# Attention into a channel-mixing block: unread products, one early load, and a third issuer of DMAs at the start

## The chip, the cores and the metric

The kernel runs on one core of a Trainium2 chip. The metric is the device time of one execution in microseconds (us). Before the change three runs gave a median of 1044.69 us (1044.38 to 1045.98). All times of rows below come from one profiled execution of the same program.

## The reference, cut to what matters

Four batches, 12 heads, 448 tokens, 64 channels a head. Scores are mixed over the heads by a 12x12 matrix ahead of the softmax, and the probabilities by another one behind it. What comes out goes through a low-rank token mixing and a two-layer channel mixing of width 3072.

```
scores = einsum('bhij,hg->bgij', q @ k.T / 8, w_pre)      # B=4, H=12, S=448, D=64
attn   = softmax(scores, axis=-1)
attn   = einsum('bhij,hg->bgij', attn, w_post)
x      = (attn @ v) as (B, S, 768)
u      = x + (x.T @ U @ V).T                              # rank 32
out    = u + relu(u @ w_ch1) @ w_ch2                      # 768 -> 3072 -> 768
```

## The kernel before, in words

The attention is cut into 17 units (`UNITS`): a unit holds some tokens of one batch, ten tokens to a chunk. The units of batch 0 have 6, 6, 12, 12 and 9 chunks; they are numbered from 0, so the "third unit" is unit 2. The work of one unit goes through these steps, and each name is that of the step in the code:

- `q` and `k` are loads. Units 0 and 1 have small q tiles (unit 0 in two loads, unit 1 in one); from unit 2 on there are two loads of three head pairs each. The k of batch 0 comes in three loads, `("k", 0, 0)`, `("k", 0, 2)` and `("k", 0, 4)`.
- `qk` multiplies q and k (line 435). For units 0 and 1 one step does four heads, so a unit has three steps; from unit 2 on a step does two heads and a unit has six.
- `qk_out` copies the scores from the PSUM bank to SBUF (lines 340 or 342, on ScalarE or VectorE).
- `relay` is a DMA, one for each head of a unit (line 456). It takes the rows of one head and spreads them over every twelfth partition of the tile `t`, so that the heads of one token lie in neighbouring partitions. There are two tiles `t`; units 0 and 2 share one, unit 1 has the other. GpSimd clears the first partitions of both at the start (line 396).
- `premix` multiplies `t` by the head matrix (line 495), two chunks to a step, so units 0 and 1 have three steps each (0 to 2 and 3 to 5), and unit 2 begins with step 6. A premix needs all twelve relays of its unit.
- `max` (VectorE), `exp` (ScalarE), `eps` (GpSimd), `recip` (VectorE) and `scale` (GpSimd) make the softmax and the scaled second head matrix; `postmix` (line 531) applies it, `post_out` copies, and `av` (lines 572 and 580) multiplies by v.

Behind the attention come the low-rank step, then the channel mixing in seven products for each 2x2 block (line 1026) and the last matmuls (line 1134).

A planner (`Plan.order`) writes down the order of every engine's instructions when the program is built. Each step has a rank, the steps that it needs, the slots that it holds, and the engines that may run it with a cost for each. The planner steps through its own time; a free engine takes the ready step of lowest rank, and where several engines may run a step, it goes to the one that would end it first. The program then has, on every engine, the order that came out. The constants of `RANK` are in units of chunks: premix step k has rank 2k. `k0` and `kstep` set the ranks of `qk` of units 0 and 1, and through these the ranks of their loads, copies and relays.

Before the change the relays of unit 0 may be issued by SP or by ScalarE (`SHARED = 1`), those of all other units by SP alone. The two q loads of unit 2 have ranks of -8.3 and -3.3 and need premix step 0.

`warm` are products of a zeroed tile with itself that nobody reads (line 484): a first block of three (`WARM[0]`), ahead of the first `qk`, and a second of five behind the last `qk` of unit 1, ahead of premix step 0. The tile `blank` is zeroed by VectorE (line 486). A float32 product of 448 columns is two matmul instructions in the trace, so the blocks have 6 and 10.

Of the kernel before, what the change touches and what calls it, by code (L numbers as in the profile page):

```python
# [18 lines left out]
B, H, S, D = 4, 12, 448, 64  # L19
# [13 lines left out]
QA, QW = 4, 124  # L33
# [11 lines left out]
class Unit:  # L45
# [10 lines left out]


RANK = dict(
    e0=-97.289, estep=7.59, er=4.323, qk_lead=4.915, qk_step=0.84, av_off=3.794, av_step=0.935, post=4.408,
    kr=0.705, vr=1.125, qr=6.14, mx=0.587, ex=0.852, ep=1.625, po=3.145, qo=1.135, uv0=6, uvs=-0.052, uv1=2.315,  # L60
    raw=5.564, k0=-12.826, kstep=0.571, m0=12.258, pu=1.842, ev=29.543, lead=14.607, t0=-4.815, ts=0.56,
    t1=2.158, ta=31.914, tb=3.344, dl=32.545, hl=13.674, out=3,
)

# [3 lines left out]


SHARED = 1  # L70
WARM = 3, 5
WEIGHT = {("POOL", "ACT"): 1.0, ("POOL", "DVE"): 3.221, ("DVE", "POOL"): 0.8, ("ACT", "DVE"): 1.3}


# [16 lines left out]
def words(ap):  # L91
    return ap.bitcast(I32).rearrange("p (n t) -> p n t", t=2)
# [165 lines left out]
def build(tc, q2, kt, vj, wpre_in, wpost_in, u_in, v_in, ident, w1j, w2, out, show=None):  # L258
# [5 lines left out]
    def pool(ctx, name, bufs, side="left", **kw):  # L264
        sb[name] = Pool(ctx.enter_context(tc.tile_pool(name=name, bufs=1, side=side, **kw)), plan.where)
        return sb[name]
# [5 lines left out]
    plan = Plan({**BUFS, **CAPS, "t": 2}, CAPS, 4, WEIGHT)  # L272
# [12 lines left out]
    p = pool(uv_ctx, "c", 1)  # L285
# [86 lines left out]
    def OUT(n):  # L372
        return [("ACT", 55 + 0.833 * n), ("DVE", 75 + 1.042 * n)]
# [7 lines left out]
    chunks, first = [], {}  # L381
# [17 lines left out]
    def rank_qk(u, h):  # L399
        if u == 0:  # L400
            return RANK["k0"] + h * RANK["kstep"]
        if u == 1:
            return RANK["k0"] + (h + 12) * RANK["kstep"]
        return first[u] - RANK["qk_lead"] - (11 - h) * RANK["qk_step"]

    def rank_av(u, p):
        return first[u + 1] + RANK["av_off"] + p * RANK["av_step"]
# [29 lines left out]
    def lent(u, p):  # L437

        n = sum(H // 2 // units[v].pairs for v in range(u)) + p // units[u].pairs
        return n if n < 9 else None  # L440
# [18 lines left out]
    for u, un in enumerate(units):  # L459
        b, size = un.b, 128 * (H // 2) * un.cols  # L460
        src = q2[at:at + size].rearrange("(p h i) -> p h i", p=128, h=H // 2)
        at += size
        at_q, hold = [], [("qk", 0, 4)] if u == 1 else []
        for p, n in Q_LOADS[min(u, 2)]:
            at_q += [p] * n
            plan.add(("q", u, p), [("SP", (430, 200 * n * un.cols // QW))], partial(load_q, u=u, p=p, n=n, src=src), rank_qk(u, 2 * p) - RANK["qr"], [("premix", first[u - 2] // 2)] if u > 1 else (), [("q", u)])
        for p in range(0, H // 2, un.pairs):
            r = rank_qk(u, 2 * p)
            o, s = ("qk", (u, p)), [("s", (u, p))] if lent(u, p) is None else []
            plan.add(("qk", u, p), [("PE", 760)], partial(qk, u=u, p=p), r, [("q", u, at_q[p]), *hold, *{("k", b, x) for x in (([p // 2 * 2]) if b == 0 else range(p, p + 1))}],  # L470
                     [o, ("q", u), ("k", b)])
            plan.add(("qk_out", u, p), OUT(2 * S), partial(qk_out, u=u, p=p), r + RANK["qo"], [("qk", u, p)], [o] + s, port=())
            for h in range(2 * p, 2 * (p + un.pairs)):
                cost = (800, 1000 * un.n // H)
                plan.add(("relay", u, h), [("SP", cost)] + [("ACT", cost)] * (u < SHARED), partial(relay, u=u, h=h), r + RANK["qo"], [("qk_out", u, p)], s + [("t", u)])


    def blank():
        return sb["xn"].tile([JP, NJ, LW], F32R, "xh", ("xn", "blank")).bitcast(F32).rearrange("p j n -> p (j n)")
# [3 lines left out]
        for _ in range(n):  # L483
            eng.matmul(o[:64, 0, :S], lhsT=z[:, S:S + 64], rhs=z[:, :S], start=True, stop=True)

    plan.add("blank", [("DVE", 700)], lambda eng: eng.memset(blank(), 0.0), -30, (), [("xn", "blank")])
    for i, n in enumerate(WARM):
        plan.add(("warm", i), [("PE", 760 * n)], partial(warm, i=i, n=n), (-30, -1)[i], ["blank"] + [[], [("qk", 1, 4), ("qk", 0, 4)]][i], [("pre", ("warm", i)), ("xn", "blank")])

# [51 lines left out]
    for k in range(NC // 2):  # L541
        r = 2 * k
        us = sorted({chunks[2 * k][0], chunks[2 * k + 1][0]})
        pre, post, st, e, wr = ("pre", k), ("post", k), ("st", k), ("e", k), ("wr", k)
        ts = [("t", u) for u in us]
# [8 lines left out]
        for js in ([(0, 1)] if len(us) == 1 else [(0,), (1,)]):  # L554
            u = chunks[2 * k + js[0]][0]
# [40 lines left out]
    for u, un in enumerate(units):  # L596
# [3 lines left out]
        for p in range(0, H // 2, AV):  # L600
            r = rank_av(u, p)
# [226 lines left out]
    for b in range(B):  # L828
        us = of_batch[b]
        RB = first[us[-1] + 1] + RANK["uv0"]  # L830
        for k in range(KC // 2):
            r = RB + 2 * RANK["uvs"] * k
            tp, tr, hp, xn, t3 = ("lr", ("tp", b, k)), ("lr", ("tr", b, k)), ("lr", ("hp", b, k)), ("xn", (b, k)), ("t3", (b, k))
# [20 lines left out]
    def when(F, p, j):  # L854
        return U0 + PU * (7 * nth[F, p] + POS[j])
# [32 lines left out]
    for p in range(2):  # L888
        b0, b1 = 2 * p, 2 * p + 1
        gates = [[None] + ["open_qk"] * 3 + ["open_t1"] * 2 + ["open_mix"], ["open_tail", "open_x1", "open_x0", "open_uv", "open_uv", "open_x2", "open_x3"]][p]  # L890
        for i in range(3):
            lo, hi = i, i + 3
            u = {(x, y): [("keep", (b0, b1)[y], (lo, hi)[x] // 2)] for x in range(2) for y in range(2)}
# [57 lines left out]
    for F in range(NF):  # L951
        r = [when(F, 0, j) - RANK["lead"] for j in range(7)]
# [3 lines left out]
        for i, f, h, j in pieces:  # L956
            key = ("w", F, i)
            src = words(w1j[2 * F + f][:, h * HW:(h + 1) * HW])
# [86 lines left out]
    for n, (F, p) in enumerate(chains):  # L1045
# [8 lines left out]
        ev = [when(F, p, j) - RANK["ev"] for j in range(7)]  # L1054
        q, s, c11, = ("hs", (n, "q")), ("hs", (n, "b")), ("hs", (n, "a"))
# [19 lines left out]
    def due(f, b, c=0):  # L1075
        return D0 + GS * group[f] + 2 * PU * (3 * b + c / 2)
# [19 lines left out]
    for f in range(KF):  # L1096
        for b in range(B):
            r = due(f, b) - RANK["hl"]
# [10 lines left out]
        for i in range(2):  # L1109
            key = ("v", f, i)  # L1110
            r = due(f, 0, 4 * i) - RANK["dl"]
            k, ka = 7 * NF + 2 * f + i, 5 * NF + 2 * f + i
            src = words(w2[f * 128:(f + 1) * 128, :][:, i * HW:(i + 1) * HW])
# [29 lines left out]
    for g, fs in enumerate(GROUPS):  # L1143
        for b in range(B):
            n = 1 if (g, b) == (NGR - 1, B - 1) else 2
            for c in range(0, KC, n):
                r = due(fs[0], b, c)
# [83 lines left out]
```

## Time and profile before

| | |
|---|---|
| median of three runs | 1044.69 us |
| profiled execution | 1043.51 us |
| its span, first to last instruction | 1041.7 us |
| TensorE busy | 1002.3 us, 96% |
| VectorE, ScalarE, GpSimd busy | 790.3, 467.5, 356.4 us |
| mean granted TensorE clock | 0.995 |

The profiled execution took 1.8 us beside its span. The busy share of TensorE is a mean: it is 74% to 88% in the six stretches of ten us from the start, and 99% from 500 us on. The table is read with that in mind: what a change at the start is worth is seen in the first 60 us.

### The profile page before, as it was taken

How to read it: one execution, taken by the hardware profiler on the slowest of the kernel's cores; microseconds unless marked ns; L12 is line 12 of the kernel's file. 1: busy time of each engine (PE TensorE's matmuls, PEld its weight loads, DVE VectorE, ACT ScalarE, POOL GpSimd, SP SyncE). 2: the span in 40 equal slices, each digit the busy share in tenths (PEclk: the TensorE clock that was granted, in tenths of full speed). 3: DMA queues.
4: the chain of work that ended last, by engine and by line, in shares of the span. 5: the costliest groups of instructions: out<-in, count | busy, mean ns of one | idle time of the engine just before them, and what ended most of it. 6: DMA issues, size and time to landing. Idle time of an engine off the chain costs nothing.

```text
span 1041.7 us, 28885 instructions
## 1 busy us (share of the span) xinstructions
PE 1002.3 (96%) x12044; PEld 840.2 (81%) x12044; DVE 790.3 (76%) x1194; ACT 467.5 (45%) x970; POOL 356.4 (34%) x461
## 2 busy tenths in 40 slices
PE   7889999999899897999999999999999999999998
PEld 2566666666566686989999999999999999999997
DVE  3375685687676779799999987894999999996223
ACT  2667767777777763444433333431333333420000
POOL 4121121223211675655565543450432413422000
PEclk9899999999999999999999999999999999999999
DMA  5755657677574233344544544686353454440023
GB/s 177 235 160 183 192 187 203 199 240 215 170 244 153 62 107 120 109 143 151 151 152 148 160 136 136 202 277 241 101 171 117 131 181 139 151 140 1 1 83 130
DMA packets 89499, 161.34 MB, mean 155 GB/s; under 512 B 10696, under 2 KB 72088, under 8 KB 89368
## 3 DMA queue, kind: packets, MB, share of 16 engines
q1 hardware_dynamic: 88948, 158.84, 47.9%
q8 instruction: 95, 1.56, 0.6%
q10 hardware_dynamic: 420, 0.65, 0.2%
q14 instruction: 36, 0.29, 0.1%
HBM read 86.14 MB, written 34.60 MB: 116 GB/s over the span
## 4 chain that ended last, share of the span: by engine, by line
PE 58%; DVE 4%; ACT 0%; issue 0%; ACTq 0%; DVEq 0%
PE bank L1134 33%; PE bank L1026 25%; DVE aw L720 1%; DVE aw L721 0%; DVE acc L875 0%; DVE x L726 0%; DVE u L347 0%; DVE aw L875 0%; DVE aw L716 0%; DVE x L725 0%; DVE hs L1039 0%; DVE acc L822 0%; DVE w L347 0%; DVE hs L342 0%; DVE xl L347 0%
## 5 line engine op out<-in xcount | busy, mean ns | idle before, releaser
L1134 PE MATMUL bank<-u,w 128*128 128x448 f32 x1728 | 345.9, 362 | 0.0
L1134 PEld LDWEIGHTS bank<-u,w 128*128 128x128 f32 x1728 | 324.0, 187 | 21.6
L1026 PE MATMUL bank<-u,w 128*128 128x448 f32 x1512 | 307.0, 364 | 7.6 <-DVE hs L1039 2.9
L1026 PEld LDWEIGHTS bank<-u,w 128*128 128x128 f32 x1512 | 284.0, 188 | 28.6 <-POOL w L347 3.3
L1137 DVE TENSOR_TENSOR acc<-acc,bank 128x896 f32<-128x896 f32 (+1 forms) x99 | 104.3, 1054 | 78.5 <-PE bank L1134 78.4
L730 POOL TENSOR_TENSOR aw<-aw,x 128x384 f32<-128x384 f32 x74 | 83.4, 1126 | 205.9 <-DVE x L726 202.2
L347 POOL TENSOR_TENSOR w<-aw,w 128x384 fp32r<-128x384 f32 x84 | 99.0, 1185 | 90.7 <-ACT w L340 88.6
L531 PEld LDWEIGHTS bank<-wr,e 60*64 60x64 f32 x5040 | 91.1, 136 | 44.3 <-issue 30.6
L507 ACT ACTIVATE e<-bank,st 128x448 f32<-128x448 f32 x180 | 113.1, 638 | 26.6 <-DVE st L513 13.0
L502 DVE TENSOR_REDUCE st<-bank 128x2 f32<-128x896 f32 x90 | 97.4, 1085 | 33.7 <-PE bank L495 32.5
L340 ACT CAST w<-aw 128x384 fp32r<-128x384 f32 x102 | 52.1, 515 | 140.9 <-PE bank L1134 68.3
L709 ACT ACTIVATE x<-kr 128x384 f32<-128x384 f32 x82 | 45.6, 556 | 127.2 <-DMA kr<-in_w 99.1
L531 PE MATMUL bank<-wr,e 60*64 60x60 f32 x5040 | 94.1, 220 | 8.2 <-issue 5.9
L435 PE MATMUL bank<-k,q 64*64 64x448 f32 (+1 forms) x768 | 92.9, 549 | 5.8 <-DMA q<-in_q 2.5
L495 PE MATMUL bank<-t,wpre 64*64 64x448 f32 x720 | 86.8, 546 | 8.6 <-DMA v<-in_vj 2.6
L510 POOL TENSOR_SCALAR st<-st 128x2 f32<-128x2 f32 x90 | 17.9, 199 | 189.4 <-ACT e L507 188.4
L340 ACT COPY hs<-bank 128x448 f32<-128x448 f32 x87 | 46.3, 534 | 74.5 <-PE bank L1026 70.0
L1094 DVE SCALAR_TENSOR_TENSOR u<-hs,u 128x448 fp32r<-128x448 f32 x96 | 78.9, 852 | 0.0
L340 ACT COPY a<-bank 128x840 f32<-128x840 f32 (+1 forms) x72 | 60.5, 845 | 35.2 <-PE bank L531 35.2
L721 DVE SCALAR_TENSOR_TENSOR aw<-x,aw 128x384 f32<-128x384 f32 x88 | 67.5, 767 | 6.6
L572 PEld LDWEIGHTS bank<-a,v 128*64 128x64 f32 x1224 | 57.4, 139 | 13.5 <-ACT a L340 4.2
L726 DVE SCALAR_TENSOR_TENSOR x<-kr,x 128x384 f32<-128x384 uint32 (+2 forms) x99 | 64.1, 647 | 3.4
(72 smaller groups left out, 1019.2 us busy)
## 6 DMA issues: line engine op xcount, KB each, us to landing
hd<-hs SPq DMA_DIRECT2D x96, 224.0 KB
hs<-hd SPq DMA_DIRECT2D x96, 224.0 KB
t<-s SPq DMA_DIRECT2D x102, 210.0 KB
kr<-in_w1j SPq DMA_DIRECT2D x48, 384.0 KB
kr<-in_w SPq DMA_DIRECT2D x48, 384.0 KB
v<-in_vj SPq DMA_DIRECT2D x24, 256.0 KB
q<-in_q SPq DMA_DIRECT2D x30, 186.0 KB
ud<-acc SPq DMA_DIRECT2D x12, 448.0 KB
```

Source lines behind the costliest of these rows:

```text
L340: eng.copy(out=o, in_=i)
L347: eng.tensor_tensor(out=o, in0=a, in1=b, op=ALU.subtract)
L435: eng.matmul(o[at, i, :S], lhsT=q[d, pj, of], rhs=k[d, pj, :], start=True, stop=True)
L495: eng.matmul(o[64 * j:64 * j + 64, i, :S], lhsT=wpre[64 * i:min(64 * i + 64, QW)], rhs=tt[side(u)][64 * i:min(64 * i + 64, QW), n, :], sta ...
L502: eng.tensor_reduce(out=mx, in_=T["pre", k][:, :, :S], axis=AX.X, op=ALU.max, negate=True)
L507: eng.activation(out=e[:, i], in_=T["pre", k][:, i, :S], func=ACTF.Exp, bias=T["mx", k][:, i:i + 1], accum_out=sm[:, i:i + 1])
L531: eng.matmul(d, lhsT=e[64 * j:64 * j + HALF, i, x * KB:x * KB + KB], rhs=wr[64 * j:64 * j + HALF, i].rearrange("p (g m) -> p g m", m=MH), ...
L730: eng.tensor_tensor(out=f32(a), in0=f32(a), in1=f32(x), op=ALU.add)
L1026: eng.matmul(o, lhsT=w[:, x, i * 128:(i + 1) * 128], rhs=u[:, i, y, :], start=j < 2 and i + t == 0, stop=i + t == 4, skip_group_check=True)
L1094: eng.scalar_tensor_tensor(out=h[:, 1, :], in0=T["hr", f, b], scalar=0.0, in1=f32(h[:, 0, :]), op0=ALU.max, op1=ALU.subtract)
L1134: eng.matmul(ps[:, j, :S], lhsT=w[:, x, cc * 128:(cc + 1) * 128], rhs=h, start=(i == 0), stop=(i == len(todo) - 1))
L1137: eng.tensor_tensor(out=two(b, c, n), in0=two(b, c, n), in1=T.pop(("dn", g, b, c))[:, :n, :S], op=ADD)
```

## The change

Three things at the start of the program, and a few constants of the planner:

- The blocks of unread products have two and three products in place of three and five, and only the 512 columns of `blank` that they read are zeroed, in place of 1024.
- The q loads of unit 2 get the rank just behind the relays of unit 0's last four heads, and need `qk_out` of these heads in place of premix step 0.
- The relays of units 1 and 2 may be issued by GpSimd too, at a cost of 1050 ns to the planner (SP's is 800).
- `k0` and `kstep` move the ranks of `qk` of units 0 and 1 from -12.8 ... -1.4 to -8.5 ... 0.2. The ranks of the first loads follow, and with these the order in which SP asks for them: q of unit 1 and the head matrix now stand ahead of the first and the second k load.
- `av_step`, `ex` and `po` shift the ranks of `av`, `exp` and `post_out` by 0.011 a pair, 0.006 and 0.039.

```diff
-    ... av_off=3.794, av_step=0.935, post=4.408,
-    kr=0.705, vr=1.125, qr=6.14, mx=0.587, ex=0.852, ep=1.625, po=3.145, qo=1.135, ...
-    raw=5.564, k0=-12.826, kstep=0.571, ...
+    ... av_off=3.794, av_step=0.924, post=4.408,
+    kr=0.705, vr=1.125, qr=6.14, mx=0.587, ex=0.858, ep=1.625, po=3.106, qo=1.135, ...
+    raw=5.564, k0=-8.529, kstep=0.437, ...
...
-WARM = 3, 5
+BY_POOL = 1, 2
+WARM = 2, 3
...
-            plan.add(("q", u, p), ..., rank_qk(u, 2 * p) - RANK["qr"], [("premix", first[u - 2] // 2)] if u > 1 else (), [("q", u)])
+            plan.add(("q", u, p), ..., rank_qk(0, 11) + RANK["qo"] + 0.01 if u == 2 else rank_qk(u, 2 * p) - RANK["qr"],
+                     [("premix", first[u - 2] // 2)] if u > 2 else [("qk_out", 0, 4)] if u == 2 else (), [("q", u)])
...
-                plan.add(("relay", u, h), [("SP", cost)] + [("ACT", cost)] * (u < SHARED), ...
+                plan.add(("relay", u, h), [("SP", cost)] + [("ACT", cost)] * (u < SHARED) + [("POOL", (1050, cost[1]))] * (u in BY_POOL), ...
...
-    plan.add("blank", [("DVE", 700)], lambda eng: eng.memset(blank(), 0.0), ...
+    plan.add("blank", [("DVE", 400)], lambda eng: eng.memset(blank()[:, :S + 64], 0.0), ...
```

## Rows read from the trace of the kernel before

**Rows 1.** The page: TensorE's busy time, and the last chain's shares by engine.
```profile
PE 1002.3 (96%) x12044; PEld 840.2 (81%) x12044; DVE 790.3 (76%) x1194; ACT 467.5 (45%) x970; POOL 356.4 (34%) x461
...
PE 58%; DVE 4%; ACT 0%; issue 0%; ACTq 0%; DVEq 0%
```

**Rows 2.** Waits of TensorE, 0 to 60 us: us in total, times, longest.
```profile
PE bank L495 <- DMA v<-in_vj: 2.6, 1, 2.6
PE bank L435 <- DMA q<-in_q: 2.5, 1, 2.5
PE bank L495 <- DMA t<-acc: 2.1, 1, 2.1
```

**Rows 3.** The same view, 60 to 420 us, its largest entry.
```profile
PE bank L531 <- issue: 4.4, 7, 1.6
```

**Rows 4.** Timeline to 20 us: start, duration (us), instructions, idle time before and releaser.
```profile
0.72 9.08 POOL L396 MEMSET t<- 4x5376 f32 x2 [0.29 <-POOLq L1219]
...
1.01 0.91 DVE L486 MEMSET xh<- 112x1024 f32 x1 [1.01 <-PEq L1219]
...
1.98 4.74 PE L484 MATMUL bank<-xh 112*64 112x448 f32 x6 [1.98 <-DVE xh L486]
...
2.28 0.70 SPq L418 DMA_DIRECT2D q<-in_q  x1
...
6.65 1.34 PE L435 MATMUL bank<-k,q 64*64 64x448 f32 x8
...
8.51 4.26 PE L435 MATMUL bank<-k,q 64*64 64x448 f32 x40 [0.53 <-DMA k<-in_kt]
...
8.99 12.09 SPq L456 DMA_DIRECT2D t<-acc  x13
9.00 6.04 ACTq L456 DMA_DIRECT2D t<-acc  x6
...
12.71 3.97 PE L484 MATMUL bank<-xh 112*64 112x448 f32 x10
...
18.78 2.49 PE L495 MATMUL bank<-t,wpre 64*64 64x448 f32 x24 [2.10 <-DMA t<-acc]
```

**Rows 5.** Timeline from 20 to 46 us.
```profile
21.12 0.95 SPq L418 DMA_DIRECT2D q<-in_q  x2
...
23.75 2.59 PE L435 MATMUL bank<-k,q 64*64 64x448 f32 x16 [2.48 <-DMA q<-in_q]
...
24.89 0.91 ACT L340 COPY acc<-bank 124x896 f32<-124x896 f32 x1 [0.76 <-PE bank L435]
...
26.10 1.72 PE L531 MATMUL bank<-wr,e 60*64 60x60 f32 x56
...
26.77 5.29 SPq L456 DMA_DIRECT2D t<-acc  x6
...
27.58 1.84 PE L435 MATMUL bank<-k,q 64*64 64x448 f32 x16
...
29.25 0.99 PE L531 MATMUL bank<-wr,e 60*64 60x60 f32 x56
...
32.81 5.29 SPq L456 DMA_DIRECT2D t<-s  x6
...
43.80 2.17 PE L495 MATMUL bank<-t,wpre 64*64 64x448 f32 x16 [2.59 <-DMA v<-in_vj]
```

**Rows 6.** Busy time by stretches of 1 us; last: granted clock, DMA share, GB/s.
```profile
4.00:5.00 1.00, 1.00 (x2) 0.23 (x1) 0.00 (x0) 0.00 (x0) 1.00 (x1) 1.00 1.01 355
...
17.00:18.00 1.00, 0.00 (x0) 0.00 (x0) 0.00 (x0) 0.00 (x0) 0.00 (x0) 1.00 0.61 212
...
26.00:27.00 1.00, 1.00 (x40) 0.90 (x36) 0.00 (x0) 0.61 (x1) 0.00 (x0) 0.50 0.49 142
```

**Rows 7.** The same view, stretches of 10 us.
```profile
20.00:30.00 10.00, 7.52 (x156) 4.08 (x152) 4.25 (x7) 6.88 (x16) 1.74 (x6) 0.83 0.60 180
...
40.00:50.00 10.00, 7.41 (x143) 4.31 (x135) 2.85 (x5) 6.05 (x13) 0.48 (x2) 0.83 0.91 272
```

More of the change, by code (lines that the diff above doesn't have):

```diff
@@ L58 @@
 RANK = dict(
-    e0=-97.289, estep=7.59, er=4.323, qk_lead=4.915, qk_step=0.84, av_off=3.794, av_step=0.935, post=4.408,
-    kr=0.705, vr=1.125, qr=6.14, mx=0.587, ex=0.852, ep=1.625, po=3.145, qo=1.135, uv0=6, uvs=-0.052, uv1=2.315,
-    raw=5.564, k0=-12.826, kstep=0.571, m0=12.258, pu=1.842, ev=29.543, lead=14.607, t0=-4.815, ts=0.56,
+    e0=-97.289, estep=7.59, er=4.323, qk_lead=4.915, qk_step=0.84, av_off=3.794, av_step=0.924, post=4.408,
+    kr=0.705, vr=1.125, qr=6.14, mx=0.587, ex=0.858, ep=1.625, po=3.106, qo=1.135, uv0=6, uvs=-0.052, uv1=2.315,
+    raw=5.564, k0=-8.529, kstep=0.437, m0=12.258, pu=1.842, ev=29.543, lead=14.607, t0=-4.815, ts=0.56,
     t1=2.158, ta=31.914, tb=3.344, dl=32.545, hl=13.674, out=3,
@@ L465, in build @@
             at_q += [p] * n
-            plan.add(("q", u, p), [("SP", (430, 200 * n * un.cols // QW))], partial(load_q, u=u, p=p, n=n, src=src), rank_qk(u, 2 * p) - RANK["qr"], [("premix", first[u - 2] // 2)] if u > 1 else (), [("q", u)])
+            plan.add(("q", u, p), [("SP", (430, 200 * n * un.cols // QW))], partial(load_q, u=u, p=p, n=n, src=src), rank_qk(0, 11) + RANK["qo"] + 0.01 if u == 2 else rank_qk(u, 2 * p) - RANK["qr"],
+                     [("premix", first[u - 2] // 2)] if u > 2 else [("qk_out", 0, 4)] if u == 2 else (), [("q", u)])
         for p in range(0, H // 2, un.pairs):
@@ L474, in build @@
                 cost = (800, 1000 * un.n // H)
-                plan.add(("relay", u, h), [("SP", cost)] + [("ACT", cost)] * (u < SHARED), partial(relay, u=u, h=h), r + RANK["qo"], [("qk_out", u, p)], s + [("t", u)])
+                plan.add(("relay", u, h), [("SP", cost)] + [("ACT", cost)] * (u < SHARED) + [("POOL", (1050, cost[1]))] * (u in BY_POOL), partial(relay, u=u, h=h), r + RANK["qo"], [("qk_out", u, p)], s + [("t", u)])
     def blank():
@@ L484, in warm @@
             eng.matmul(o[:64, 0, :S], lhsT=z[:, S:S + 64], rhs=z[:, :S], start=True, stop=True)
-    plan.add("blank", [("DVE", 700)], lambda eng: eng.memset(blank(), 0.0), -30, (), [("xn", "blank")])
+    plan.add("blank", [("DVE", 400)], lambda eng: eng.memset(blank()[:, :S + 64], 0.0), -30, (), [("xn", "blank")])
     for i, n in enumerate(WARM):
```

## The prediction

> **What bounds the kernel now.** I read the page first, for the engine that is the limit and for where the last chain goes, then the waits of TensorE, then the timeline around the largest of them, then stretches for the clock and the transfers. TensorE is busy 96% of the span and carries 58% of the last chain, VectorE 4% [rows 1]: whatever lets TensorE do the same work earlier shows in the end time. In the first 60 us three waits for transfers stand out, 2.1, 2.5 and 2.6 us [rows 2]; from there to 420 us no entry is over 4.4 us, and that one is seven pieces of at most 1.6 [rows 3]. The edits lie at those three waits.
>
> The timeline tells what they are. TensorE ends the unread products and waits 2.10 us for the relays of unit 0 (premix 0 at 18.78). It ends the three premixes at 21.27 and waits 2.48 us for q of unit 2, which SP asked for only at 21.12, behind thirteen relays from 8.99 on [rows 4, 5]. And it waits 2.59 us ahead of the first premix of unit 2 at 43.80 [rows 5]. The releaser named there is a v load, but a premix reads no v; it reads `t`, so what is late is unit 2's relays, issued by SP from 26.77 to 38.10.
>
> Two more things have a price. In the two stretches of ten us that hold the waits of 2.48 and 2.59 us, the granted clock is 0.83 [rows 7]: 1.7 us each at the level of 1.2 GHz. The first is seen in the work: sixteen qk matmuls take 2.59 us where the next sixteen take 1.84, and a postmix 1.72 us where the next takes 0.99 [rows 5], 1.48 us together. And while relays run alone the DMA engines are busy 0.61 of 16, at 212 GB/s; loads reach 1.01 and 355 GB/s [rows 6]. A relay writes ten partitions, and 0.61 of 16 engines is ten: these ten are near full.
>
> **The change part by part.** All times are against the profiled run, 1043.51 us (span 1041.7 and 1.8 beside it), which is 1.2 us under the median of 1044.69.
>
> *The q loads of unit 2.* Behind six relays of unit 0 at 12.09/13 = 0.93 us each, SP comes to them at 8.99 + 5.6 = 14.6 in place of 21.12. They landed 2.6 us behind the issue before (23.75 - 21.12); even if their packets queue behind unit 0's last relay, to 18.78, they are there 2.6 - 0.95 later, at 20.5, ahead of the end of the premixes. So the 2.48 us go, hidden behind the premixes. What is late next is the chain max, exp, scale: with qk of unit 2 earlier, TensorE comes to postmix 0 earlier and may wait there.
>
> *Relays of unit 1 by GpSimd.* GpSimd is free when its two memsets end at 9.80 [rows 4]. No row shows a DMA issued by GpSimd. From below I bound an issue by SP's 5.29/6 = 0.88 us [rows 5], from above by twice ScalarE's 6.04/6 = 1.01 [rows 4], and take 1.01, the nearest issue by an engine that also computes. SP then has about six relays of unit 1 in place of twelve, 5 us less, and is no longer late for unit 2: the copy for its first relay ended at 24.89 + 0.91 = 25.80 and SP issued it at 26.77 [rows 5]. That is 0.97 us, and it goes.
>
> The other side: relays of unit 1 begin while unit 0's are in flight, now out of a third queue. From the first copies of unit 1, about 13, to the landing of unit 0's last relay ahead of 18.78, ScalarE's six had half of ten engines nearly full. With a third sharer, what is left of them, some 4 us, may take half as long again at worst: 0 to 2 us on premix 0. I take 0.7.
>
> The Trainium skill speaks against the change here (DMA: Bandwidth & Descriptors, Issuing engines are not separate DMA queues): DMAs of SP, ScalarE and GpSimd run on the same 16 engines and interleave, so several issuers save issue time only. The 0.61 that holds while two queues issue agrees. By the rule alone, the gain is that of the transfer-bound rival below; by the row on SP's late issue, it is mine.
>
> *Relays of unit 2 by GpSimd.* SP needed 11.3 us for twelve; two issuers need half, so issue is no longer the limit, and the transfers are. Of the 2.59 us ahead of premix 6, between 0 (transfers bound) and all may go. I take 1.0, since the stretch at 26 us has the engines at 0.49 [rows 6]: a fifth of their time was free for want of issues.
>
> On GpSimd, `eps` and `scale` now queue behind relays that wait for a `qk_out`. Each relay in front of them delays a postmix by an issue (1.01) or more. I cost it at nothing: until 43.80 TensorE has the wait for unit 2's relays as cover. If that goes, one or two such delays come to 1 to 2 us.
>
> *Order of the first loads.* q of unit 1, 192 KB, goes ahead of the first k load, at the 355 GB/s of this time [rows 6] 0.55 us. The second and third k have the same bytes ahead of them as before. So qk starts later, but the next qk, waiting for k at 8.51 [rows 4], does not. Bounds 0 and 0.55; I take 0.3, for the first relays leave later.
>
> *Unread products and memset.* One product less ahead of qk and a memset half as long free TensorE from its first block at about 4.7 in place of 6.7 (4.74 us for six matmuls, 0.79 each, two fewer, and 0.45 us sooner [rows 4]), but k lands no sooner: no gain. The pace of 0.79 against 3.97/10 = 0.40 in the second block is that of the lower clock. With less work ahead, qk may run at it for longer: 1.34 us for eight matmuls against 0.85 (4.26/5 [rows 4]), 0.5 us each for two or three steps. It hides behind the issue of unit 0's relays, which have 5.6 us of issue from the first on; without that cover it is 1 to 1.5 us. The second block is 1.6 us shorter (two products of 0.79), so the wait ahead of premix 0 grows from 2.10 to 3.7 us. Behind 2.10 us idle the premixes ran at full pace, 24 in 2.49 us; behind 2.48 us the clock fell. So I let the first 1.48 us of slow work move from qk to the premixes and gain nothing by it. Bounds: a gain of 1.48 or a loss of 1.
>
> *Small ranks.* Shifts of under 0.04 chunks swap few neighbours. I cost them at nothing, with 1.6 us either way, the longest piece of rows 3.
>
> The sum: -2.48 - 0.97 + 0.7 - 1.0 + 0.3 = -3.45 us, 1040.1 for the profiled run, and 1041.2 for the median. Behind 44 us the shift is passed on, since what follows waits on TensorE or on steps that move with it.
>
> **The rivals.**
>
> *Transfer-bound, no change.* The ten engines carry all relays of units 0 to 2 almost without a break; earlier issues only lengthen their queue. For it: 0.61 during relays, and 0.60 as the mean of 20 to 30 us. Against it: 0.49 at 26 us. Then only the free fifth of about four such microseconds is won, 0.8 us, and the 0.3 of the first loads goes off: 1044.2.
>
> *Spread over more engines.* GpSimd's relays use DMA engines beyond those ten, so transfers end sooner, and both waits (2.48, 2.59) and the second slow stretch (1.7) go, less 0.3 and half of the 0.7: -6.1 us, 1038.6. For it: 0.39 of the engines stand idle while relays run. Against it: the relays of both present issuers stay within 0.61 together.
>
> The Trainium skill has such a rule (DMA: Bandwidth & Descriptors, Why a DMA increments its semaphore by 16 and not by 1): a hardware-generated copy takes the lowest-numbered engines, one by GpSimd's software consecutive ones from a cursor that moves round. The 0.61 agrees with the first half; no row shows the second.
>
> *GpSimd too slow, a loss.* It takes about six relays of each unit from about 12.6 on, in order. SP's last relay of unit 2 left at 38.10; twelve by GpSimd end later than that from (38.10 - 12.6)/12 = 2.1 us each on. At 2.5 us they end at 42.6, and premix 6 and all behind it are 4.5 us later: 1049.2. For it: a relay of unit 2 carries twice the rows of one of unit 1, and the wait for a `qk_out` adds to the issue. Against it: 0.88 and 1.01 on the other two.
>
> **How the numbers follow.** Forecast 0.46, with its own range 1039.2 to 1043.2; spread 0.20; transfer-bound 0.20; GpSimd too slow 0.14. A measurement of this kernel tells 0.2%, 2.1 us, from no change. Faster: 0.41 of the forecast's 0.46, the 0.20 of the spread and 0.03 of the transfer-bound case, 0.64. Slower: 0.14 and 0.02 of late reorderings, 0.16. Same: 0.20. The range takes in the spread with a little more of the clock, and half of the loss: 1037.5 to 1046.0.
>
> **What would show it.** Right: q of unit 2 issued by SP at about 15 and no wait behind the premixes; premix 0 at 19 to 20; the first relay of unit 2 at the end of its copy; the first premix of unit 2 at about 40 to 41. Wrong: that premix still at 43 or later with the DMA engines at 0.6 until then (transfer-bound); DMA share over 0.7 while relays run alone (spread); GpSimd's issues over 2 us each, or postmix waiting for `scale` in a row of steps (too slow); the 3.5 us there at 44 us and gone at 400 (order).

## The result: slower by half a per cent

The changed kernel took a median of 1047.79 us in 20 runs, the kernel before 1042.38 us in 20; the ratio is 1.0054 (95% interval 1.0028 to 1.0080). The forecast was 1041.2 us and faster: 3.45 us less than the 1044.69 it was counted from, where the two medians here lie 5.4 us the other way. Single executions of either program spread by more than the difference (1037.28 to 1051.33 before, 1042.35 to 1055.68 after), so below the verdict on a time comes from the interval, and the verdict on a mechanism from the trace. The profiled execution after took 1046.92 us, its span is 1045.1.

The timeline of TensorE in the changed kernel, to 56 us, in the columns of [rows 4]:

```profile
1.45 3.25 PE L486 MATMUL bank<-xh 112*64 112x448 f32 x4 [1.45 <-DVE xh L488]
6.70 6.62 PE L436 MATMUL bank<-k,q 64*64 64x448 f32 x48 [2.00 <-DMA k<-in_kt]
13.26 2.47 PE L486 MATMUL bank<-xh 112*64 112x448 f32 x6
24.85 1.77 PE L497 MATMUL bank<-t,wpre 64*64 64x448 f32 x8 [9.13 <-DMA q<-in_q]
...
51.74 3.27 PE L497 MATMUL bank<-t,wpre 64*64 64x448 f32 x16 [0.29 <-DMA t<-s]
```

The two lines to compare are the premixes. Premix 0 starts at 24.85 where it was 18.78 [rows 4]: TensorE waits 9.13 us for it, in place of 2.10. The first premix of unit 2 starts at 51.74 where it was 43.80 [rows 5]. Part of that comes back. The 22nd `max` is the same step in both kernels; its line in the timeline of VectorE is, before:

```profile
100.56 1.09 DVE L502 TENSOR_REDUCE st<-bank 128x2 f32<-128x896 f32 x1 [0.69 <-PE bank L495]
```

and after:

```profile
104.54 1.09 DVE L504 TENSOR_REDUCE st<-bank 128x2 f32<-128x896 f32 x1 [0.69 <-PE bank L497]
```

It is 4.0 us late. From there on the shift of the `max` steps goes between 2.5 and 6.0; at about 335 us it is 4.1, and the spans differ by 3.4. So the loss is made in the first 60 us and then, in the main, passed on.

What premix 0 waits for is in the queues. From 16 to 25 us the DMA queues of the kernel before (packets, MB, share of 16 engines; q1 is SP's, q10 ScalarE's):

```profile
q1 hardware_dynamic: 986, 1.46, 53.0%
q10 hardware_dynamic: 131, 0.20, 6.6%
```

and of the changed kernel, with GpSimd's queue q0:

```profile
q0 software_dynamic: 274, 0.64, 36.1%
q1 hardware_dynamic: 529, 0.75, 29.6%
q10 hardware_dynamic: 159, 0.24, 13.2%
```

The same bytes moved, 1.66 and 1.63 MB. But 0.64 MB were GpSimd's: its six relays of unit 1, which no step waited for yet. ScalarE's queue holds only relays of unit 0, for which premix 0 waits, and all of them were issued by 15.35. Before, it had no packet from 18 us on; after, it still moved eight between 22 and 23 us and two between 23 and 24:

```profile
q10 hardware_dynamic: 8, 0.01, 4.2%
...
q10 hardware_dynamic: 2, 0.00, 0.7%
```

The releaser named at 24.85 is a load of q, but a premix does not read q; as with the v load at 43.80 [rows 5], the name is only that of a transfer that ended just before. The trace's semaphore records tell which ended last of those that premix 0 needs: ScalarE's last relay is complete at 24.45, SP's last of unit 0 at 23.23.

The same view counts the packets by size, before and after:

```profile
DMA packets 1117, 1.65 MB, mean 184 GB/s; under 512 B 152, under 2 KB 1117, under 8 KB 1117
```

```profile
DMA packets 962, 1.63 MB, mean 181 GB/s; under 512 B 249, under 2 KB 844, under 8 KB 962
```

The 118 packets over 2 KB are GpSimd's. Each is 5376 B, three rows of a relay; a relay that SP or ScalarE issued moves in packets of one row, 1792 B.

GpSimd's own part was quick. Its timeline, and then its lines in the list of DMA issues (KB each, median us to landing):

```profile
13.55 2.42 POOL L457 DMA_DIRECT2D t<-acc  x4 [3.73 <-DVE acc L343]
16.59 1.10 POOL L457 DMA_DIRECT2D t<-acc  x2 [0.62 <-ACT acc L341]
```

```profile
t<-acc POOLq DMA_DIRECT2D x6, 105.0 KB, 8.6
t<-s POOLq DMA_DIRECT2D x3, 210.0 KB, 8.7
t<-acc POOLq DMA_DIRECT2D x2, 210.0 KB, 5.4
```

An issue takes 0.55 to 0.61 us, less than on SP; the median landing takes 5.4 to 8.7 us.

### The profile page after: what moved, and what is told of

It reads as the page before. It is cut to its first block, busy times and chain, and to the rows that moved or that the text cites. A ratio compares the mean times of both kernels' runs of the same rounds, so it can differ in the third digit from the quotient of the medians.

```text
span 1045.1 us, 28904 instructions
## 1 busy us (share of the span) xinstructions
PE 1001.9 (96%) x12038; PEld 840.9 (80%) x12038; DVE 793.9 (76%) x1197; ACT 464.4 (44%) x969; POOL 361.0 (35%) x470
## 4 chain that ended last, share of the span: by engine, by line
PE 58%; DVE 4%; ACT 0%; issue 0%; ACTq 0%; DVEq 0%
PE bank L1136 33%; PE bank L1028 25%; DVE aw L722 1%; DVE aw L723 0%; DVE acc L877 0%; DVE x L728 0%; DVE u L348 0%; DVE aw L877 0%; DVE aw L718 0%; DVE x L727 0%; DVE hs L1041 0%; DVE acc L824 0%; DVE w L348 0%; DVE hs L343 0%; DVE xl L348 0%
## 5 line engine op out<-in xcount | busy, mean ns | idle before, releaser
L1028 PEld LDWEIGHTS bank<-u,w 128*128 128x128 f32 x1512 | 284.5, 189 | 27.9 <-POOL w L348 3.3
L533 PEld LDWEIGHTS bank<-wr,e 60*64 60x64 f32 x5040 | 90.5, 135 | 44.4 <-issue 27.9
L497 PE MATMUL bank<-t,wpre 64*64 64x448 f32 (+1 forms) x720 | 90.2, 558 | 13.4 <-DMA q<-in_q 9.1
L574 PE MATMUL bank<-a,v 128*64 128x120 f32 (+4 forms) x1224 | 64.1, 258 | 4.2 <-issue 2.9
```

The source lines that it names most:

```text
L497: eng.matmul(o[64 * j:64 * j + 64, i, :S], lhsT=wpre[64 * i:min(64 * i + 64, QW)], rhs=tt[side(u)][64 * i:min(64 * i + 64, QW), n, :], sta ...
L533: eng.matmul(d, lhsT=e[64 * j:64 * j + HALF, i, x * KB:x * KB + KB], rhs=wr[64 * j:64 * j + HALF, i].rearrange("p (g m) -> p g m", m=MH), ...
L574: eng.matmul(main[i * D:(i + 1) * D, c, :n], lhsT=v[:, p + c, i, x, :], rhs=a[:, x * H + 2 * (p + c) + i, :n], start=(c == 0 and x == 0), ...
L1028: eng.matmul(o, lhsT=w[:, x, i * 128:(i + 1) * 128], rhs=u[:, i, y, :], start=j < 2 and i + t == 0, stop=i + t == 4, skip_group_check=True)
```

## The experiments

Three accounts were set against each other. Crowding: GpSimd's relays of the next unit take the DMA engines from the relays that the present unit waits for. Early q: the loads of q do that. Products and constants: fewer unread products, or a new order, lose the time. "Over before" is the ratio to the kernel before with its interval.

**Without GpSimd.**

```diff
-BY_POOL = 1, 2
+BY_POOL = ()
```

> The changed kernel with GpSimd taken out of the issuers; q of unit 2 early, fewer unread products and the new constants stay. Crowding theory (GpSimd's relays of unit 1 take the DMA engines from unit 0's last relays, which ScalarE issued): premix 0, at 18.8 us before and 24.9 after, starts at 19 to 20.5, and the whole is 2 to 4 us under the kernel before. Rival 1 (the early q loads do it, ahead of those relays on the engines): premix 0 still at 23 or later, the whole 3 to 6 us over before. Rival 2 (fewer unread products and new order): premix 0 at 19 to 20, but the whole still 3 to 6 us over before, with the clock low behind it.

Premix 0 at 19.07, as crowding has it; 1.0025 over before (0.9996 to 1.0054), where it wanted 2 to 4 us less. Its trace shows another wait, ahead of premix 3, the first of unit 1, which started at 30.82 us before:

```profile
19.07 0.99 PE L497 MATMUL bank<-t,wpre 64*64 64x448 f32 x8 [3.83 <-DMA q<-in_q]
...
34.45 4.76 PE L497 MATMUL bank<-t,wpre 64*64 64x448 f32 x24 [2.08 <-DMA t<-acc]
```

So the late premix 0 is GpSimd's doing, and the rest of the change is not the gain that I forecast. This order has a fault of its own, found further below: SP's last relay of unit 1 stands behind four of unit 2.

**GpSimd for unit 2 alone.**

```diff
-BY_POOL = 1, 2
+BY_POOL = (2,)
```

> The changed kernel with GpSimd as an issuer for unit 2 alone. Crowding: unit 0's relays are alone again, so premix 0 starts at 19 to 20.5, unit 2's relays by two issuers land no later than without GpSimd, and the whole is 2 to 5 us under the kernel before. Rival 1 (early q): premix 0 at 23 or later. Rival 2 (products and order): as in the run without GpSimd, 3 to 6 us over before. If GpSimd's transfers are slow in themselves, wherever they stand, the first premix of unit 2 comes 2 us or more later than in the run without GpSimd.

1.0067 over before (1.0042 to 1.0092), where crowding wanted a gain of 2 to 5 us: that part of the expectation missed. Premix 0 at 21.73; this execution had its k 1.7 us later than the run above, so its later steps are measured from premix 0. The first premix of unit 1 came 17.3 us behind it (38.98), without GpSimd 15.4; the first of unit 2 29.8 (51.48), without GpSimd 27.2 (46.26). The sign that the last outcome of the expectation names came true. Whether GpSimd's transfers are slow in themselves or hold up others is not told by it. SP's last relay of unit 1 left with four of unit 2 ahead of it in both runs (two of SP's and two of GpSimd's here); the first premix of unit 1 came 7.1 us behind that issue, without GpSimd 4.7.

**GpSimd's issues, but a sixth and a twelfth of its bytes.**

```diff
-    eng.dma_start(out=tt[side(u)][QA + h::H][:, :n], in_=T["s", u, p][r:r + MC * n, h % 2])
+    if eng is nc.gpsimd:
+        eng.dma_start(out=tt[side(u)][QA + h::H][:, :1], in_=T["s", u, p][r:r + MC * n:n, h % 2])
+    else:
+        eng.dma_start(out=tt[side(u)][QA + h::H][:, :n], in_=T["s", u, p][r:r + MC * n, h % 2])
```

> The changed kernel in its own order, in which each relay issued by GpSimd moves one chunk of its 6 or 12 (the other chunks of these heads are left as cleared; the two memsets clear the whole of t). Every issue and wait stays, only GpSimd's traffic goes, to 1/6 and 1/12. Crowding: premix 0 at 19 to 20.5 in place of 24.9, and unit 2's first premix 4 us or more earlier than in the changed kernel. If it is the early q, the order or the issue itself: premix 0 at 23 or later.

The order of all engines is that of the changed kernel, instruction for instruction. The waits are not: the last two of unit 1's three copies wait here until thin relays of GpSimd have landed, at 19.07 and 22.27 in place of 13.14 and 15.39. So GpSimd had issued one relay by 20.4 us, where the changed kernel had issued six by 17.7:

```profile
14.48 0.73 POOL L458 DMA_DIRECT2D t<-acc  x1 [4.65 <-DVE acc L343]
...
19.07 1.09 DVE L343 COPY acc<-bank 128x896 f32<-128x896 f32 x1 [5.21 <-DMA t<-acc]
...
23.46 2.06 POOL L458 DMA_DIRECT2D t<-acc  x4 [2.47 <-ACT acc L341]
```

Queues from 16 to 25 us, then the premixes:

```profile
q1 hardware_dynamic: 742, 1.08, 40.7%
q10 hardware_dynamic: 177, 0.27, 9.7%
q0 software_dynamic: 94, 0.05, 2.3%
```

```profile
20.83 1.09 PE L500 MATMUL bank<-t,wpre 64*64 64x448 f32 x8 [4.47 <-DMA t<-acc]
...
45.31 1.74 PE L500 MATMUL bank<-t,wpre 64*64 64x448 f32 x16 [0.18 <-DMA t<-s]
```

Premix 0 comes 4.0 us earlier than in the changed kernel and the first premix of unit 2 6.4 us, the span is 1039.1 in place of 1045.1 (one execution). Without GpSimd's traffic ahead of premix 0 most of its delay is gone, though the early q loads are still there. Whether it is the bytes alone, or also that five of the six relays were issued later, this run does not tell. Premix 0 was expected by 20.5; the 0.3 us above that, and what is left to 18.78, also has the first relays 0.9 us later (they need the longer clearing here).

**GpSimd alone, on the kernel before.**

```diff
-[("SP", cost)] + [("ACT", cost)] * (u < SHARED), ...
+[("SP", cost)] + [("ACT", cost)] * (u < SHARED) + [("POOL", (1050, cost[1]))] * (u in BY_POOL), ...
```

> The kernel before, with GpSimd as an issuer of relays of units 1 and 2 and nothing else of the change. Crowding: premix 0 at 23 to 25 in place of 18.8, and the whole 2 to 6 us over before. Rival 1 (early q): premix 0 at 18.8 to 20 and the whole within 2 us of before. Rival 2: the same as rival 1.

1.0043 over before (1.0015 to 1.0070), and the line to look at is:

```profile
23.70 4.76 PE L496 MATMUL bank<-t,wpre 64*64 64x448 f32 x24 [7.08 <-DMA t<-acc]
```

Premix 0 is 4.9 us late, its 24 matmuls take 4.76 us in place of 2.49 [rows 4], and here the releaser named is a relay. No load of unit 2's q is issued here before 23.06. GpSimd as an issuer, alone, gives nearly the whole of the change's loss.

**The early q alone, on the kernel before.**

```diff
-rank_qk(u, 2 * p) - RANK["qr"], [("premix", first[u - 2] // 2)] if u > 1 else ()
+rank_qk(0, 11) + RANK["qo"] + 0.01 if u == 2 else rank_qk(u, 2 * p) - RANK["qr"],
+[("premix", first[u - 2] // 2)] if u > 2 else [("qk_out", 0, 4)] if u == 2 else ()
```

> The kernel before, with the early q loads of unit 2 and nothing else. In this order qk of unit 2 stands between and ahead of the premixes of unit 0. If the wait for q was worth what it lasted: premix 0 at 18.8 to 20, no wait for q, the whole 2 to 3 us under before. Rival (the early q draws qk and its copies ahead of the softmax of unit 0, and only reorders): the third premix of unit 0 at 23 or later in place of 20.4, and the whole within 1 us of before or up to 3 us over. If early q crowds the engines by itself: premix 0 at 22 or later.

1.0001 over before (0.9973 to 1.0028). TensorE now has two qk steps of unit 2 ahead of premix 0, and premix 0 starts at 22.27, the third premix at 26.82; TensorE waits 3.7 us for q ahead of these qk steps and 4.2 us ahead of the first premix of unit 2, at 46.00. The rival came true: the wait was moved, nothing was won.

**What is left: products, constants, order of the first loads.**

```diff
-BY_POOL = 1, 2
+BY_POOL = ()
```

(and the q loads as before)

> The changed kernel without GpSimd as an issuer and without the early q: what is left is fewer unread products, the shorter clearing, the new constants and the order of the first loads. Crowding theory: within 1.5 us of the kernel before. Rival (products and constants cost): 2 to 5 us over before, seen as a low clock in the premixes of unit 0 or as a shift that grows behind 60 us.

1.0032 over before (1.0003 to 1.0060), so a cost of its own, against the crowding account as I had put it. The premixes:

```profile
19.36 3.68 PE L496 MATMUL bank<-t,wpre 64*64 64x448 f32 x24 [3.90 <-DMA t<-acc]
...
35.67 1.77 PE L496 MATMUL bank<-t,wpre 64*64 64x448 f32 x8 [4.49 <-DMA t<-acc]
```

Premix 3 is 4.9 us late. In the order that the planner wrote, SP issues eleven relays of unit 1, then four of unit 2, of twice the bytes, and only then the last of unit 1. In the run without GpSimd it is the same; in the next run two of unit 2 stand ahead of it.

**The early q with TensorE's order held.**

```diff
-at_q, hold = [], [("qk", 0, 4)] if u == 1 else []
+at_q, hold = [], [("qk", 0, 4)] if u == 1 else [("premix", 2)] if u == 2 else []
```

> The kernel before with the early q loads, and qk of unit 2 made to need premix 2, so that TensorE's order stays premixes first, as before. If only the wait for q is taken out: qk of unit 2 starts behind the third premix without a wait, at about 21.3 in place of 23.8, and the whole is 2 to 3 us under before. Rival (what is late next takes it, unit 1's or unit 2's relays on SP): the first premix of unit 1 or of unit 2 starts no earlier than before, and the whole is within 1 us of it.

1.0027 over before (1.0000 to 1.0053). qk of unit 2 starts at 22.57 without a wait, 1.2 us earlier than before. The first premix of unit 2 starts at 44.03, no earlier than 43.80 [rows 5]. Of the rival, that came true; the whole is 2.8 us over, not within 1. The place of the wait is another than it named: unit 2's relays left sooner (25.2 to 36.3, before 26.8 to 37.2), the premix has no wait, and TensorE waits 2.30 us for `exp` ahead of a postmix:

```profile
36.37 2.84 PE L532 MATMUL bank<-wr,e 60*64 60x60 f32 x112 [2.30 <-ACT e L508]
```

**GpSimd without the early q.**

```diff
-rank_qk(0, 11) + RANK["qo"] + 0.01 if u == 2 else rank_qk(u, 2 * p) - RANK["qr"], ...
+rank_qk(u, 2 * p) - RANK["qr"], [("premix", first[u - 2] // 2)] if u > 1 else (), ...
```

> The changed kernel without the early q loads; GpSimd still issues relays of units 1 and 2. Crowding by GpSimd's relays: premix 0 at 23 to 25, and the whole 3 to 7 us over the kernel before, no better than the changed kernel. If the early q takes part in the crowding: premix 0 at 20 to 22.5 and the whole 2 to 3 us under the changed kernel.

1.0037 over before (1.0007 to 1.0066), premix 0 at 22.04. The early q takes part: premix 0 is 2.8 us later with it (24.85), and 1.2 us later than with GpSimd alone (23.70), one execution each. The whole is not apart from the changed kernel by these intervals.

**k0 and kstep alone, on the kernel before.**

```diff
-k0=-12.826, kstep=0.571
+k0=-8.529, kstep=0.437
```

> The kernel before with the new k0 and kstep alone, so with the new order of the first loads; SP's order of relays stays as before. Theory (what the products and constants cost is the relays' order on SP: the last relay of unit 1 behind four of unit 2): nothing here, premix 0 at 18.8 to 19.5 and the whole within 1.5 us of before. Rival (q of unit 1 and the head matrix ahead of k cost): premix 0 at 20 or later and 2 to 4 us over.

1.0007 over before (0.9981 to 1.0032), premix 0 at 19.42: no cost that can be told.

**Fewer products and the shorter clearing alone.**

```diff
-WARM = 3, 5
+WARM = 2, 3
```

(and the smaller memset)

> The kernel before with fewer unread products and the shorter clearing alone; unit 1's relays all stand ahead of unit 2's. Theory (relay order): within 1.5 us of before, though the premixes of unit 0 may run at the low clock. Rival (fewer products cost, through the clock): premixes of unit 0 at half pace, 3.5 us or more for 24 matmuls in place of 2.5, and the whole 2 to 4 us over before.

1.0020 over before (0.9988 to 1.0052): inconclusive by time. The premixes of unit 0 take 4.13 us in place of 2.49, but premix 3 is at 30.16 (30.82 before), so that delay is gone by then.

**Unit 2's relays with a twelfth of their bytes, in the order of before.**

```diff
+if u == 2:
+    eng.dma_start(out=tt[side(u)][QA + h::H][:, :1], in_=s[0:MC * n:n])
```

> The kernel before in its own order, in which the relays of unit 2 move one chunk of twelve (the others are left as cleared; the memsets clear the whole of t). If the transfers of unit 2's relays set its first premix (43.8 us before, behind a wait of 2.6): that premix starts 2.5 us or more earlier and without the wait. If the work ahead of it on TensorE and the softmax set it: 43 or later, and the wait comes back as another one.

The first premix of unit 2 starts at 42.44 and has no wait; the start of this execution is 1.4 us late (premix 0 at 20.21), so from premix 0 on it is 22.2 us in place of 25.0. The wait of 2.59 us is one for transfers. That 2.8 us are all that can be had is not shown: a copy of unit 2 waits here 2.21 us for a thin relay, at 30.93, and TensorE 1.20 us for that copy, which the kernel before does not do:

```profile
31.89 0.98 PE L499 MATMUL bank<-t,wpre 64*64 64x448 f32 x8 [1.20 <-ACT acc L340]
```

**All relays of unit 1 ahead of unit 2's.**

```diff
+    plan.lines.append([("relay", u, h) for u in (1, 2) for h in range(H)])
     order = plan.order()
```

(on the kernel with products and constants alone)

> Fewer products and the new constants, without GpSimd and the early q, as in the run of these alone (premix 3 at 35.7 us there, 1.0032 of before), with one thing added: SP has all relays of unit 1 ahead of those of unit 2. Theory (relay order): premix 3 at 31 to 33, and the whole within 1.5 us of the kernel before. Rival (products, constants): premix 3 at 31 to 33 too, but the whole still 2 to 4 us over before.

0.9993 over before (0.9964 to 1.0022). The premixes of units 0 and 1:

```profile
18.91 4.18 PE L496 MATMUL bank<-t,wpre 64*64 64x448 f32 x24 [2.10 <-DMA t<-acc]
29.23 0.98 PE L496 MATMUL bank<-t,wpre 64*64 64x448 f32 x8
```

Premix 3 comes 6.4 us earlier than with the one relay behind, so the delay of premix 3 was that order. The whole goes from 1.0032 to 0.9993, but the two intervals overlap, and by time alone the two are not told apart. The changed kernel itself does not have this order: there SP's six relays of unit 1 stand ahead of all of unit 2's. GpSimd as an issuer is therefore left as the main cause of its loss, and alone it costs 1.0043. That it does so by crowding is shown at premix 0 by the queues and by the two runs with GpSimd's relays out of the way; how the loss splits between units 1 and 2 is open. No version of these is faster than the kernel before by more than the measurement tells.

## Why the prediction was wrong, step by step

*Relays of unit 1 by GpSimd: the step that failed.* The mechanism was named and its size was off. I bounded the delay of premix 0 by 0 to 2 us and took 0.7; it was 6.07, and 4.9 with GpSimd alone. I counted a third queue as one sharer more of the same kind. From 16 to 25 us GpSimd's queue moved 0.64 MB, in packets of 5376 B, and ScalarE's, whose relays were issued first, 0.24 MB in packets of 1792 B. In the trace's records one of GpSimd's packets took 0.43 us on average, one of ScalarE's 0.14, before the change 0.085. In which order the engines serve the queues no run tests. I also counted ScalarE's remaining relays as 4 us of work; its last relay was complete at 24.45, 11 us behind GpSimd's first issue at 13.55. The early q adds to it, 1.2 to 2.8 us by the runs above; the prediction had that at nothing, without a reason.

The rule of the Trainium skill that I had against the change (DMA: Bandwidth & Descriptors, Issuing engines are not separate DMA queues) held: with a third issuer the same 1.6 MB moved in the same nine microseconds, so no bandwidth was gained. Gain by it would have needed SP's issue to be the limit, and loss followed since the bytes came in the wrong order.

*The q loads of unit 2.* The wait for q is gone from its old place, as forecast, but not its 2.48 us: alone the ratio is 1.0001, and 1.0027 with TensorE's order held. In the changed kernel they left at 16.14 and the first was complete at 24.7, where I had 14.6 and 20.5. I passed the shift on to 43.80. In the first of the two runs unit 2's relays left later (27.9 to 38.1) and its first premix waited 4.2 us; in the second TensorE waited for `exp`, the chain that I had named as late next and given no price. My rival of transfers, with a gain of 0.8 us in all, was nearer on this term.

*SP late for unit 2 (0.97 us).* Not won. After the late premix 0, qk of unit 2 ran from 26.37 and SP's first relay of unit 2 left at 32.08, in place of 26.77 [rows 5]. The copy was not what it waited for. Units 0 and 2 share a tile `t`, so this relay needs premix 2, the last of unit 0, which ran from 31.00 to 31.98. The waits of SP's queue from 26 to 45 us:

```profile
SPq L457 <- PE bank L497: 3.3, 1, 3.3
```

This is how the late premix 0, and qk of unit 2 between the premixes, reach unit 2. The prediction has no term for it.

*Relays of unit 2 by GpSimd (1.0 us).* Not won. The run with unit 2 alone has the first premixes of units 1 and 2 later by 2 to 3 us, measured from premix 0; it has the relay order of the run without GpSimd with two of SP's exchanged for GpSimd's, so the part of the issuer is not clean.

*GpSimd's price of issue.* 0.55 to 0.61 us, under my lower bound of 0.88. The rival on the slow side had the sign right and the mechanism wrong: GpSimd issues quickly, and what it issues lands late.

*Spread over more engines.* My sign for it came, the gain did not. From 16 to 25 us the DMA share is 0.79, over the 0.61 of before (with the q loads in it), but at 181 GB/s against 184: more packet time, no more bytes. A share is no measure of engines in use here: from 16 to 17 us it is 1.25, so packet times overlap.

*First loads and small ranks.* The second k load also has the head matrix, 31 KB, ahead of it now, which I had overlooked. First relays at 9.46 in place of 8.99, 0.47 us, in the bounds of 0 to 0.55; k0 and kstep alone are 1.0007. The three small constants alone leave the order of every engine as it was, so their cost is nothing.

*Unread products.* Right in kind: in the run of these alone the low clock moved to the premixes (24 matmuls in 4.13 us), and the time is not told from no change.

## What to carry to other kernels

Here a third issuer let transfers that nobody needed yet overtake those that the next step waited for; where the DMA engines are near full, ask what a new issuer's transfers will delay, and try giving it the urgent ones (no run here did). Before a wait is booked as a gain, look at what the next step downstream waits for, buffers included: the 2.5 us for q came back as waits for relays or for `exp`, and unit 2's relays could not start before unit 0 had left their tile. When bytes are taken out of a run to test a cause, compare the times of the issues as well, since new waits can move them. When a planner writes the order, a new rank can put one small transfer behind four large ones, so read the order that came out of it.

## What the runs showed of the hardware that I had not expected

Single executions have pauses of TensorE of about 2 us in the middle of a block, with no releaser, at other places in each execution. Behind some of them the granted clock falls to its level of 1.2 GHz; behind one of 2.25 us in the changed kernel, at 192.9 us, it did not. In the run with thin relays of unit 2, the timeline of TensorE and the stretch around it:

```profile
100.79 2.53 PE L576 MATMUL bank<-a,v 128*64 128x120 f32 x29 [2.03 <-issue]
```

```profile
100.00:105.00 5.00, 4.21 (x61) 3.34 (x65) 0.45 (x2) 0.83 (x3) 0.58 (x2) 0.66 0.02 6
```

The block had begun at 98.13 with 7 of its 36 matmuls. The pause and the 0.66 of clock over five microseconds cost 2.0 + 1.7 us, and the 22nd and 23rd `max` went from 3.0 us ahead of the kernel before to 0.8 behind. Just ahead of it, at 98.46, a transfer of 16 KB of the instruction queue (q8) had begun. In all kept traces together there are 20 pauses of 1.6 us or more without a releaser, the first 6 us left out; 19 of them begin from 0.35 us ahead of the start of such a transfer to 1 us behind it, a stretch in which about a quarter would fall by chance. Whether the pauses come from these transfers no run tests. One such event is as large as the effects studied here; it is part of the spread of single executions, and a shift read from one trace has to be followed to the stage where it was made.
